# Thresholds of a build-time scheduler set for each period, and the last rows of x transposed on TensorE, in an attention kernel

## The chip, the cores and the metric

The kernel runs on one core of one Trainium2 chip. The time is that of the device in microseconds (us); a profile, taken in one execution, has a span from the first to the last instruction, which is a little shorter than the time. Engines are named as in the profile: PE is TensorE (PEld its weight loads), DVE is VectorE, ACT is ScalarE, POOL is GpSimd, SP is SyncE, which here only issues transfers.

## The reference

Two attention blocks over the same input are mixed by a gate. Block A is full attention with 32 heads of 16 over 2048 rows; block B looks only at 8 earlier rows, two apart.

```python
x = A_x                                            # 1 x 2048 x 512, bf16
g = sigmoid((x * gate_w).sum(-1, keepdims=True))
# block A: q, k, v = x @ wqkv, 32 heads of 16
scores = einsum("bhqd,bhkd->bhqk", q, k) * 16 ** -0.5
a = (softmax(scores) @ v) @ A_wo
# block B: window of W = 8, dilation 2
idx = pos[:, None] - arange(8)[None, :] * 2        # masked where negative
b = (softmax(q . k[idx]) . v[idx]) @ B_wo
return g * a + (1 - g) * b
```

Block A has 32 x 2048 x 2048 scores, each of which needs an exponential. That is the bulk of the work.

## The kernel before

The program is written by a small planner that runs while the kernel is built. It keeps a time for each engine, estimates how long each step takes, and emits each instruction at the moment when its plan would start it. On the chip each engine then runs its own list in this order. The planner's thresholds therefore decide the order of instructions, and nothing else.

Block A is cut into 32 periods: 4 chunks of 512 queries times 8 groups of 4 heads. A period has 64 units; a unit is one head, 128 keys, 512 queries. TensorE writes scores of 3 or 2 units by turns into a ring in PSUM, ScalarE exponentiates the ring into `pT`, and TensorE adds the product with v to `acc`:

```python
want = 3 if k % 2 == 0 else 2                 # units of ring k
...
def f():                                      # TensorE: the scores
    shut = acc_open[0]
    twice = (shut is not None and not any(row_left[shut])
             and P.have(P.now + dur) < TWICE * P.HAM)
    for _ in range(1 + twice):                # issued twice where TensorE would be thin
        for s_, (p_, t, j) in enumerate(units):
            qk_mm(ring[:, s_, :], p_, t, j)
    ...                                       # and a rider for DVE or POOL, if there is room
# ScalarE:
A.activation(out=st["pT"][:, 0:n, :], in_=ring[:, 0:n, :], func=ACT.Exp,
             scale=LN2 / 128.0, bias=-VOFF * LN2 / 128.0)
```

Some units ("riders") go to a PSUM bank `w` instead, and VectorE computes their exponential in four passes (`ta`, `ta`, `ta`, `pd`), or GpSimd does (`psc`). What ScalarE doesn't exponentiate, these do.

The jobs between the rings (projections of q, k and v, block B, output) may start on TensorE only if they end before ScalarE's queue runs out:

```python
refill = 0.52
RAMP = 0.01
JW = 0.8
JP = 3.0
EARLY = 0.3
TEARLY = 110

def limit(self, st):          # when ScalarE's queue runs out, less refill
    return max(self.free["act"], st) + sum(y[4] for y in self.ready["act"]) + self.coming - self.refill

def room_for_job(self, x, st):
    return not self.calm or st - x[7] > self.JP or self.dve_work(st) >= self.JW

def fits(self, x, st):
    if x[0] < 2 or self.spent or self.free["act"] + 3.0 < st or self.urgent(x):
        return True
    give = self.EARLY if st < self.TEARLY else 0.0
    return st + x[4] - self.limit(st) <= max(give, self.RAMP * (st - x[7] - self.CALM))
```

`URG = 28` tells with how many units left a job of the next period becomes urgent, `DV_MIN = 12` with how few left no rider is taken, `TWICE = 0.60` below which occupancy of TensorE a ring is issued twice at the end of a period. In gaps of TensorE the planner also puts fills: matmuls of zeros, added to `acc`, which change nothing in the result.

At the start x is needed transposed (`xT`). Three chunks of 512 rows are loaded plainly and transposed by TensorE (`s<-ident,xr`), with a copy by DVE or ACT; the fourth is loaded by a transposing transfer:

```python
load_x(8, 4)
SP.dma_start_transpose(out=xT[:, :, 3 * QW:S], in_=x2d[3 * QW:S, :])
SP.dma_start(out=wv[:], in_=a_w3[:, :, 2 * D:3 * D])
...
XDVE = ((1, 0), (1, 0), (1, 1))               # which half is copied by DVE
XARR = ((5.8, 5.8), (7.2, 7.2), (9.3, 9.3), (12.6, 12.6))    # planned arrival, us
...
v_group(0, 8, ev_start[0], 3)                 # v of heads 0 to 7, from the start of period 0
```

Then the first period needs: k of all chunks, the maximum of k (`kmax`), a selector from it (`selk`), a matmul with it, `qt`, and the first ring.

Of the kernel before, what the change touches and what calls it, by code (L numbers as in the profile page):

```python
# [20 lines left out]
NG = 8  # L21
W = 8
DIL = 2
QW = 512
# [27 lines left out]
class Plan:  # L52
# [13 lines left out]
    held = {"job": 0}  # L66
    streamed = deque()
    cap_job = 2
    refill = 0.52
    patience = 6.0  # L70

    def resource(self, name, n):
# [106 lines left out]

    DEFER = 0.0  # L180
    coming = 0.0
    RAMP = 0.01
    CALM = 4.0

    def limit(self, st):
        return max(self.free["act"], st) + sum(y[4] for y in self.ready["act"]) + self.coming - self.refill

    passes = 0
    calm = False
    JW = 0.8  # L190
    JP = 3.0
    HUNG = 0.0
    EARLY = 0.3
# [31 lines left out]
    def run(self):  # L225
        while True:
            best = None
            for e, lst in self.ready.items():
                rs = []
                for x in lst:  # L230
                    g_ = self.gate(x[6])
                    if g_ is not None:
                        rs.append(max(x[2], g_))
                if rs:
                    st = max(self.free[e], min(rs))
                    if best is None or st < best[0]:
                        best = (st, 1, e)
            for r, lst in self.reqs.items():
                if lst and self.slots[r]:
                    st = max(min(x[0] for x in self.slots[r]), min(x[2] for x in lst))  # L240
                    if best is None or st <= best[0]:
                        best = (st, 0, r)
            if best is None:
                return
            st, kind, nm = best
            self.now = st
            if kind == 0:
                lst = self.reqs[nm]
                x = min(y for y in lst if y[2] <= st + 1e-9)
                lst.remove(x)  # L250
                s = min(y for y in self.slots[nm] if y[0] <= st + 1e-9)
                self.slots[nm].remove(s)
                self.advance(x[3], st, s[1])
            else:
                lst = self.ready[nm]
                ok = [y for y in lst if y[2] <= st + 1e-9 and self.gate(y[6]) is not None
                      and self.gate(y[6]) <= st + 1e-9]
                x = min(ok, key=lambda y: (y[0], y[1]))
                if nm == "pe" and 1 <= x[0] < 1.5 and st - x[2] < self.DEFER:
                    jobs = [y for y in lst if y[0] >= 2 and y[4] > 0.5 and y[7] <= st  # L260
                            and self.gate(y[6]) is not None and self.gate(y[6]) <= st + 1e-9]
                    y = min(jobs, key=lambda y: (y[0], y[1])) if jobs else None
                    if (y is not None and st + y[4] <= self.limit(st)
                            and (y[6] != "w" or self.room_for_job(y, st))):
                        x = y
                if nm == "pe" and self.feed_dve(st):
                    continue
                if nm == "pe" and x[6] == "w" and not self.room_for_job(x, st):
                    x[2] = max(x[2], st + 0.1)
                    continue  # L270
                if nm == "pe" and not self.fits(x, st):
                    for y in ok:
                        y[2] = max(y[2], st + 0.1)
                    continue
                lst.remove(x)
                if nm == "pe":
                    self.idle_fill(st, 1 + (x[6] is not None))
                if x[6] is not None:
                    slot = self.take(x[6], st)
                    self.held["job"] += x[6] == "w"  # L280
                    more = x[5](slot)
                else:
                    more = x[5]()
                if isinstance(more, float):
                    x[4] += more
                if nm == "pe":
                    self.stream(st, x[4] - 0.116 - self.thin)
                    self.thin = 0.0
                if CFG_DEBUG:
                    LOG.append((st, x[4], nm, getattr(x[3], '__name__', '?'), x[0]))  # L290
                self.free[nm] = st + x[4]
                self.advance(x[3], st + x[4] + self.LAT[nm], None)


@with_exitstack
def kernel(
# [12 lines left out]
    x2d = A_x.flatten_outer_dims()  # L309
    out2d = out.flatten_outer_dims()  # L310
    S, D = x2d.shape
    assert D == 512 and S == 2048
    NT = S // 128
    NC = S // QW
# [41 lines left out]
    SP = Chained(nc.sync, "sp")  # L356
# [16 lines left out]
    xT = const.tile([128, DC, S], BF16, name="xT")  # L373
# [24 lines left out]
    def load_x(t0, n):  # L398
        SP.dma_start(out=xr[t0 // 8][:, t0 // 4 % 2, t0 % 4:t0 % 4 + n],
                     in_=x2d[t0 * 128:(t0 + n) * 128, :].rearrange("(t p) n -> p t n", p=128))  # L400
# [2 lines left out]
    load_x(4, 4)  # L403
    SP.dma_start(out=wqr[:, :, 0:128], in_=a_w3[:, :, 0:128])
    load_x(8, 4)
    SP.dma_start_transpose(out=xT[:, :, 3 * QW:S], in_=x2d[3 * QW:S, :])
    SP.dma_start(out=wv[:], in_=a_w3[:, :, 2 * D:3 * D])
    SP.dma_start(out=wkr[:, :, 128:D], in_=a_w3[:, :, D + 128:2 * D])
    SP.dma_start(out=wqr[:, :, 128:D], in_=a_w3[:, :, 128:D])
# [41 lines left out]
    P = Plan(["pe", "act", "dve", "pool", "sp"])  # L451
# [24 lines left out]
    QR = 2  # L476
    QRD = 2
    SOLO = 1
    TWICE = 0.60
    THIN = 0.40  # L480
    KRP = 4
    QRP = 3
    XDVE = ((1, 0), (1, 0), (1, 1))
    XARR = ((5.8, 5.8), (7.2, 7.2), (9.3, 9.3), (12.6, 12.6))
    WARR = (4.8, 8.0)
    GP = 4.5
    BB = 3
    BR = 1
    URG = 28
    TURN = 6.0  # L490

    class Bank:
# [17 lines left out]
    NP = len(periods)  # L510
    pidx = {p: k for k, p in enumerate(periods)}
    ev_x = [Event() for _ in range(NC)]
# [6 lines left out]
    ev_q = [Event() for _ in range(NP)]  # L519
    ev_start = [Event() for _ in range(NP)]  # L520
# [16 lines left out]

    def x_job(sc):
        left = [2]
        if sc == NC - 1:  # L540
            yield ("delay", XARR[sc][0])
            yield ("set", ev_x[sc])
            return
        for hf in range(2):
            yield ("spawn", x_half(sc, hf, left))

# [305 lines left out]
    nset = [0]  # L852
    ndve = [0]
    nsolo = [0]
    DV_MIN = 12
    DV_END = 7
    flying = [0]
    psc = [None]
# [54 lines left out]
    def urgent(x):  # L913

        p = front[0]
        return (p < NP - 1 and x[0] <= 4.0 + 0.3 * min(p + 1, 2 * NG) + 0.1 and rem(p) < URG
                and x[3].__name__ in ("k_job", "q_job", "kpk_job", "qpk_job", "v_job"))
    P.urgent = urgent

    def rem(p):  # L920
        return sum(len(d) for d in pend[p])

    def ready(ev, t):
        return ev.time is not None and ev.time <= t
# [86 lines left out]
    def act_stream():  # L1011
        while front[0] < NP:
# [6 lines left out]
            p = front[0]  # L1019
# [16 lines left out]
            for p_, us in parts:  # L1036
                yield ("wait", ev_q[p_])
                for t, j in us:
                    yield ("wait", ev_k[periods[p_][1]][t // TPC])
                if ev_start[p_].time is None:  # L1040
                    P.calm = 0 < p_ < NP - 1
                    yield ("set", ev_start[p_])
            if k == 0:
                next_phase("rA", "rB")
            ring = pools[rname].tile([128, 3 if k % 2 == 0 else 2, QW], FP32, tag=rname, bufs=1, name="ring")
            dur = 0.108 + MM

            def f():
                shut = acc_open[0]
                twice = (shut is not None and not any(row_left[shut])  # L1050
                         and P.have(P.now + dur) < TWICE * P.HAM)
                for _ in range(1 + twice):
                    for s_, (p_, t, j) in enumerate(units):
                        qk_mm(ring[:, s_, :], p_, t, j)
                more = MM * twice
                if (shut is not None and any(row_left[shut])
                        and P.have(P.now + dur) < THIN * P.HAM):
                    more += fill_pass(0.2134, P.now) + 0.01
                js = [u[2] for u in units]
                while len(js) < 4:  # L1060
                    r = rider(js)
                    if r is None:
                        break
                    p_, t, j, s, ds, hs = r
                    js.append(j)
                    wt = wtile(s, [128, QW])
                    qk_mm(wt[:], p_, t, j)
                    P.spawn(vec_unit(p_, t, j, s, ds, hs, wt, ndve[0]), P.now + dur + more + P.LAT["pe"])
                    ndve[0] += 1
                return float(more)  # L1070
# [7 lines left out]
        now = yield ("now",)  # L1078
# [23 lines left out]
    def rider(js, now=None):  # L1102
        now = P.now if now is None else now
        for p in (front[0], front[0] + 1):
            if p >= NP or rem(p) < (DV_MIN if p < NP - 1 else DV_END) or not ready(ev_q[p], now):
                continue
            c_, i = periods[p]
            opts = [j for j in range(4) if j not in js and pend[p][j] and ready(ev_k[i][pend[p][j][-1] // TPC], now)
# [526 lines left out]
    def v_group(h0, h1, rel, prio):  # L1635
        n = (h1 - h0) * DH
        TB = 512 // n
        for tb in range(0, NT, TB):
            P.spawn(v_job(h0, h1, tb, TB, rel, prio + 0.01 * tb))
# [12 lines left out]
        P.spawn(k_job(0, NC - 1, None, 1.5, hf))  # L1652
    P.spawn(sel_job(0, 1.5))
    P.spawn(q_job(0, None, 1.6))
    v_group(0, 8, ev_start[0], 3)
    P.spawn(act_stream())
    P.spawn(g_job(GP))
    P.spawn(psc_job(ev_lent), 16.0)
# [18 lines left out]
    for c_ in range(NC):  # L1677
        for b in range(NB):
            p = pidx[(c_, 2 * b + 2)]
# [58 lines left out]
```

## Time and profile before

| | before |
|---|---|
| time, median of 3 runs | 849.57 us (849.07 to 849.78) |
| span of the profile | 848.0 us |
| PE busy | 751.2 us, 89% |
| DVE busy | 762.1 us, 90% |
| ACT busy | 826.6 us, 97% |
| POOL busy | 725.3 us, 86% |
| mean granted clock of TensorE | 0.999 |

Busy times overlap: all engines run beside each other, and the shares are of one span. Groups of instructions are named by what they write and read, so `pT<-ring` is an exponential of a ring. A number after the arrow in square brackets, or after the second bar of a group, is the time for which the engine sat idle just before, with what ended it.

### The profile page before, as it was taken

To read this page: it belongs to the slowest core of one execution; us is meant where nothing else is said; L and a number is where in the kernel's file an instruction comes from. 1 tells how busy PE (TensorE), PEld (TensorE's weight loads), DVE (VectorE), ACT (ScalarE), POOL (GpSimd) and SP (SyncE) were. 2 spreads that over 40 slices of the span, in tenths; PEclk is the share of its full clock that TensorE was granted. 3 is DMA by queue.
4 is the path that set the end of the run, shared out by engine and by line. 5 is a ranking of instruction groups with operands and counts; after the bars stand their busy time and mean duration, and the time that the engine had idled before them with its cause. 6 is when DMAs were issued, how large, how long until landed. Compare 5 with 4: busy or idle time off the path is not lost.

```text
span 848.0 us, 15723 instructions
## 1 busy us (share of the span) xinstructions
PE 751.2 (89%) x5813; PEld 267.4 (32%) x5864; DVE 762.1 (90%) x1323; ACT 826.6 (97%) x750; POOL 725.3 (86%) x734
## 2 busy tenths in 40 slices
PE   9999998998898898888899988888888899788887
PEld 4423333342232333222323323332332332233332
DVE  4689799999999999999987899999999989999986
ACT  5999999999999999999999999999999999999996
POOL 2566798989799979899999999999999998988773
PEclk9999999999999999999999999999999999999999
DMA  9000540250434040603041414120313222020100
GB/s 272 29 2 27 167 128 12 84 172 20 131 93 151 13 137 8 180 20 111 14 144 44 131 26 131 57 69 20 106 33 112 75 83 80 20 63 7 14 1 26
DMA packets 74125, 63.84 MB, mean 75 GB/s; under 512 B 22576, under 2 KB 70704, under 8 KB 74048
## 3 DMA queue, kind: packets, MB, share of 16 engines
q1 hardware_dynamic: 72848, 62.57, 24.3%
q8 instruction: 46, 0.75, 0.4%
q10 hardware_dynamic: 1200, 0.26, 0.2%
q14 instruction: 31, 0.25, 0.1%
HBM read 45.61 MB, written 12.62 MB: 69 GB/s over the span
## 4 chain that ended last, share of the span: by engine, by line
ACT 66%; issue 20%; PE 10%; DVE 4%; POOL 0%; ACTq 0%; POOLq 0%
ACT pT L350 65%; PE w L350 4%; PE acc L350 3%; PE ring L350 3%; DVE ta L350 2%; ACT lg L350 1%; PE s L350 1%; DVE pd L350 1%; PE e L350 0%; DVE psc L350 0%; DVE xT L350 0%; DVE d L350 0%; DVE kt_all L350 0%; DVE osb L350 0%; DVE omg L350 0%
## 5 line engine op out<-in xcount | busy, mean ns | idle before, releaser
L350 ACT ACTIVATE pT<-ring 128x1536 bf16<-128x1536 f32 x718 | 817.2, 1408 | 5.2 <-PE acc L350 2.4
L350 PE MATMUL ring<-qt,kt_all 32*128 32x512 bf16 x1860 | 286.9, 381 | 83.1 <-ACT pT L350 69.1
L350 DVE SCALAR_TENSOR_TENSOR ta<-ta,w 128x512 f32<-128x512 f32 x472 | 314.4, 682 | 5.8
L350 POOL TENSOR_TENSOR prod<-prod 128x512 f32<-128x512 f32 (+1 forms) x208 | 240.2, 1166 | 5.7
L350 PE MATMUL acc<-pT,vp_all 128*17 128x512 bf16 x1795 | 221.5, 383 | 2.6 <-DVE accS L350 2.0
L350 PEld LDWEIGHTS <-kt_all 32*128 32x128 bf16 x2113 | 113.2, 91 | 334.7 <-issue 321.8
L350 PE MATMUL acc<-ident,z 128*17 128x512 bf16 (+3 forms) x770 | 193.6, 338 | 1.4 <-POOL ident masks.py:199 1.4
L350 DVE TENSOR_SCALAR ta<-w 128x512 f32<-128x512 uint16 x236 | 161.3, 687 | 37.2 <-PE w L350 35.1
L350 DVE SCALAR_TENSOR_TENSOR pd<-ta,w 128x512 uint16<-128x512 f32 x236 | 159.4, 681 | 3.0
L350 POOL TENSOR_TENSOR prod<-ksh,qb 128x512 f32<-128x512 bf16 x128 | 145.2, 1156 | 2.0
L350 POOL TENSOR_TENSOR prod<-vsh,lg 128x512 f32<-128x512 bf16 x128 | 136.5, 1098 | 2.5
L350 PE MATMUL w<-qt,kt_all 32*128 32x512 bf16 x253 | 95.0, 383 | 0.0
L350 PE MATMUL acc<-pd,vp_all 128*17 128x512 bf16 x253 | 82.0, 380 | 0.0
L350 PEld LDWEIGHTS <-z 128*17 128x17 bf16 (+1 forms) x775 | 53.4, 92 | 71.0 <-issue 43.2
L350 PEld LDWEIGHTS <-vp_all 128*17 128x17 bf16 x2048 | 41.1, 88 | 94.2 <-issue 92.9
L350 POOL TENSOR_TENSOR psc<-psc 128x512 f32<-128x512 f32 x51 | 60.8, 1193 | 3.9
L350 POOL TENSOR_SCALAR psc<-psc 128x512 f32<-128x512 uint16 (+1 forms) x34 | 21.0, 618 | 45.0 <-DVE psc L350 42.8
L350 PE MATMUL w<-bw,xT 128*128 128x512 bf16 x173 | 48.7, 382 | 1.2
L350 PEld LDWEIGHTS <-xT 128*128 128x128 bf16 x448 | 31.6, 98 | 28.1 <-issue 14.6
L350 POOL TENSOR_TENSOR lg<-lg,mx 128x256 f32<-128x256 f32 x16 | 10.1, 629 | 22.1 <-DVE mx L350 22.1
L350 DVE CAST kvs<-w 128x512 bf16<-128x512 f32 x32 | 21.9, 683 | 2.4 <-PE w L350 2.3
L350 DVE COPY accS<-acc 128x512 f32<-128x512 f32 (+1 forms) x33 | 21.9, 667 | 1.9 <-PE acc L350 1.9
(108 smaller groups left out, 447.0 us busy)
## 6 DMA issues: line engine op xcount, KB each, us to landing
ksh<-kv_scr SPq DMA_DIRECT2D x16, 1024.0 KB
vsh<-kv_scr SPq DMA_DIRECT2D x16, 1024.0 KB
kv_scr<-kvs SPq DMA_DIRECT2D x16, 256.0 KB
kt_all<-k_scr SPq DMA_DIRECT2D x6, 512.0 KB
q_scr<-qpk SPq DMA_DIRECT2D x24, 128.0 KB
qt<-q_scr SPq DMA_DIRECT2D x24, 128.0 KB
out_dram<-osb SPq DMA_DIRECT2D x14, 128.0 KB
xr<-in_A_x_dram SPq DMA_DIRECT2D x3, 512.0 KB
```

Of the source, the lines that this page charges most:

```text
L350: return chain_on(self._key, f(*a, **k))
```

## The change

The thresholds are now set anew when a period starts in the plan, from a table with one row for each of the 32 periods. The table was found by a search in the plan: a short end of the plan, with few stretches in which TensorE's occupancy is low. And the last 512 rows of x are loaded plainly, in two halves, and transposed on TensorE like the others. The first group of v no longer waits in the plan for period 0 to start.

```diff
-    refill = 0.52
+    refill = 0.4
...
-    RAMP = 0.01
+    RAMP = 0.006
...
+    TUNED = ("JW", "JP", "RAMP", "refill", "EARLY", "ahead", "least", "shy")
+    ahead = 28
+    least = 12
+    shy = 0.60
...
+STAGES = [
+    (0.8, 3.0, 0.006, 0.4, 0.3, 28, 12, 0.6),
+    (0.8, 3.0, 0.006, 0.4, 0.3, 28, 12, 0.6),
+    (0.8, 3.0, 0.006, 0.4, 0.3, 28, 12, 0.55),
...                                   # 26 rows cut
+    (1.2, 4.0, 0.01, 0.52, 0.3, 28, 10, 0.65),
+    (0.8, 3.0, 0.006, 0.52, 0.3, 36, 14, 0.6),
+    (0.8, 2.0, 0.004, 0.4, 0.3, 32, 10, 0.65),
+]
...
     load_x(8, 4)
-    SP.dma_start_transpose(out=xT[:, :, 3 * QW:S], in_=x2d[3 * QW:S, :])
+    load_x(12, 2)
+    load_x(14, 2)
...
-    XDVE = ((1, 0), (1, 0), (1, 1))
-    XARR = ((5.8, 5.8), (7.2, 7.2), (9.3, 9.3), (12.6, 12.6))
+    XDVE = ((1, 0), (1, 0), (1, 1), (0, 1))
+    XARR = ((5.8, 5.8), (7.2, 7.2), (9.3, 9.3), (9.9, 10.6))
...
-        if sc == NC - 1:
-            yield ("delay", XARR[sc][0])
-            yield ("set", ev_x[sc])
-            return
...
                 if ev_start[p_].time is None:
                     P.calm = 0 < p_ < NP - 1
+                    for nm, v in zip(P.TUNED, STAGES[min(p_, len(STAGES) - 1)]):
+                        setattr(P, nm, v)
                     yield ("set", ev_start[p_])
...
-    v_group(0, 8, ev_start[0], 3)
+    v_group(0, 8, None, 3)
```

`ahead`, `least` and `shy` stand for `URG`, `DV_MIN` and `TWICE` of before.

## The prediction

> **What bounds the kernel now.** I read first the page's busy shares, then the groups with different shapes kept apart, then ScalarE's own timeline at both ends of the span, then the waits, and last the windows for the clock.
>
> ```profile
> span 848.0 us, 15723 instructions
> PE 751.2 (89%) x5813; PEld 267.4 (32%) x5864; DVE 762.1 (90%) x1323; ACT 826.6 (97%) x750; POOL 725.3 (86%) x734
> ACT  5999999999999999999999999999999999999996
> PEclk9999999999999999999999999999999999999999
> ACT 66%; issue 20%; PE 10%; DVE 4%; POOL 0%; ACTq 0%; POOLq 0%
> ```
>
> ScalarE (ACT) is busy in every slice but the first and the last, and the chain that ended last runs through it for 66%. All engines are over 85%, but only ACT has no room.
>
> ```profile
> L350 ACT ACTIVATE pT<-ring 128x1536 bf16<-128x1536 f32 x359 | 581.8, 1621 | 3.6 <-PE ring L350 1.8 <-PE acc L350 1.3 <-PE w L350 0.5
> L350 ACT ACTIVATE pT<-ring 128x1024 bf16<-128x1024 f32 x359 | 429.4, 1196 | 1.6 <-PE acc L350 1.1 <-PE w L350 0.2 <-PE ring L350 0.2
> L350 DVE TENSOR_SCALAR ta<-w 128x512 f32<-128x512 uint16 x236 | 161.3, 687 | 37.2 <-PE w L350 35.1
> L350 POOL TENSOR_SCALAR psc<-psc 128x512 f32<-128x512 uint16 x17 | 10.5, 618 | 43.5 <-DVE psc L350 42.8
> ```
>
> One unit of attention is 128 keys of one head against 512 queries; there are 32 periods x 64 = 2048. ACT exponentiates 359 x 3 + 359 x 2 = 1795 of them, VectorE (DVE) 236 by a polynomial, GpSimd (POOL) 17. The column after the second bar is idle time just before the group: 3.6 + 1.6 = 5.2 us for the whole stream of exponentials.
>
> ```profile
> 14.51 2.56 SPq L350 DMA_DIRECT2D kv_scr<-zpad  x1
> ...
> 17.88 4.62 ACT L350 ACTIVATE pT<-ring 128x1536 bf16<-128x1536 f32 x4 [1.43 <-PE ring L350]
> ```
>
> ```profile
> 818.81 20.45 ACT L350 ACTIVATE pT<-ring 128x1536 bf16<-128x1536 f32 x18 [1.28 <-PE acc L350]
> 842.09 0.37 ACT L350 COPY oT<-e 128x256 bf16<-128x256 bf16 x1 [2.83 <-PE e L350]
> ```
>
> So the span has three parts: a head of 17.88 us before the first exponential, a stream to 818.81 + 20.45 = 839.26, that is 821.4 us, and a tail of 848.0 - 839.26 = 8.7 us. Of the 5.2 us of idle time, 1.43 lies before the first exponential, so the stream holds 3.8 us of idle: one stall of 1.28 at 818 us, and, from ACT's busy time in windows, 1.77 between 40 and 100 us (58.23 busy of 60) and about 0.7 elsewhere. The rate is (821.4 - 3.8) / 1795 = 0.4555 us per unit, small activations included.
>
> [...] ACT's 97% leaves 3.8 us of idle in 821.4[...] The trace has (1621 - 1196) / 512 = 0.83 ns per column[...]; but consecutive activations overlap, since 359 x (1621 + 1196) ns = 1011 us of records fit in 817 us. For this reason I use the 0.4555 us of the stream and not the duration of a record. [...] The granted clock here is 1.00 in every window to 830 us and 0.77 only in the last 3 us, when no matmul is left; so no run of this kernel's stream shows a drop. [...] 0.69 us per copy of 1024 columns on DVE, 1.01 on ACT.
>
> **The change, part by part.** I compared the instruction lists of both programs. Almost all counts are equal; what differs is small.
>
> *The head.* The transposing DMA of the last 512 rows goes: its issue held the SyncE queue from 3.29 for 6.47 us, so that wv was issued at 9.81 us. In its place two plain loads and 16 transposes on TensorE (16 more after the 16 of the third chunk), one copy of 1024 columns on DVE and one on ACT. Was the old transposing load on the path? No: TensorE runs from 13.25 us through the projections of k for chunks 2 and 3 without a gap.
>
> ```profile
> 11.25 1.06 PE L350 MATMUL s<-ident,xr 128*128 128x128 bf16 x16
> 12.15 2.99 PE L350 MATMUL s<-xT,wkp 128*128 128x512 bf16 x16
> 15.07 1.20 PE L350 MATMUL acc<-ident,z 128*32 128x512 bf16 x5
> ```
>
> So this adds one more batch of transposes to a busy engine: 12.15 - 11.25 = 0.90 us later. But 13.25 held a wait for DVE's copy (0.35 us), which the batch covers: +0.6 on TensorE. After this the chain is: k of the last half, its maximum on DVE, the selector, the matmul with it, qt on DVE, the first ring, ACT. The list shows two things put into that chain: 16 matmuls of v (1.07 us in the row at 17.76) now stand ahead of the selector's matmul, and the copy of v on DVE (0.6 us from start to start) stands ahead of qt. I followed it with the durations above, as an estimate: last k projection done at 15.65, last maximum at 16.4, selector 16.85, v matmuls 15.8 to 16.75 and thus beside this, selector's matmul done at 17.3, v's copy 17.0 to 17.6, qt from 17.6 instead of 16.63. qt to ACT's start took 17.88 - 16.63 = 1.25 before, so the first exponential starts at 18.85: **+1.0 us**. For the loads I see no wait: the first three were in by 11.04 and the fourth is needed only at 12.1.
>
> *The units.* DVE's polynomial count goes from 236 to 238, POOL stays at 17, ACT has one activation of 1024 columns less: 2 x 0.4555 = **-0.9 us**. DVE pays 8 passes of 0.6 from start to start (about 4.8 us of its 762), beside ACT.
>
> *The stall at 818 us.* Here two ring refills were issued twice over, and nine products with v and five fills stood ahead of the next ring. Between the ring before and the ring after, 12,288 and 11,264 matmul columns were queued, against a mean of about 7,580 for two rings. In the changed list no such heap is left late (the largest after ring 30 is 10,368). I take the whole stall off: **-1.3 us**.
>
> *The thresholds.* Refill goes from 0.52 to 0.40 in 26 of the 32 rows and RAMP from 0.01 to 0.006 in 23; in eight rows nothing else differs from the old constants, and each other column keeps its old value in 21 to 28 rows. EARLY counts only up to 110 us of the plan, where it is 0.3 as before. A smaller refill lets a projection end 0.12 us later relative to ACT's queue, and a ring takes 17.88 - 17.44 = 0.44 us from its first matmul to ACT's start: 0.40 is a little too tight, and can cost up to 0.04 us where a job just fits. The smaller RAMP takes back a part. Of the other 2.5 us of idle I let 0.4 be won: **-0.3 us** after rounding for the tight fits. Fills fall from 775 to 759 weight loads and second issues by about 5 ring matmuls: off the path.
>
> *The tail.* The matmuls left after the last ring go from 17,920 columns to 16,384, but the last steps are the same chain: 0.
>
> Sum: +1.0 - 0.9 - 1.3 - 0.3 = -1.5, so 849.57 - 1.5 = **848.1 us**.
>
> **Rivals.** *(a) The plan wins nearly all the idle.* If the search has removed the stalls that the plan can see, and the head costs less than I think because loads land early, the gain is up to 3.8 + 0.9 = 4.7 us: 844.9. For it: the change was chosen by the plan's end. Against it: ACT's gaps are few and at different places, 1.77 us of them where EARLY stays, and the head is longer by the list itself. *(b) The clock drops.* [...] ACT starves for some us at each place: 852 to 860. Against it: the clock was 1.00 throughout, and if I count distinct matmul passes against ACT's time in every stretch of four rings, the thinnest is 0.46 before and 0.51 after; the two lists are alike. *(c) TensorE becomes the bound* because jobs may run later into ACT's reserve: small waits of 0.04 to 0.1 us after some of the 718 rings. A hundred of them make +4 to +8 us: 852 to 856. For it: refill below the 0.44 measured. Against it: RAMP is smaller, and 200 rings already waited for ACT, 69.1 us in all, so TensorE is often ahead.
>
> ```profile
> PE ring L350 <- ACT pT L350: 69.1, 200, 0.6
> ACT pT L350 <- PE acc L350: 2.4, 4, 1.3
> ACT pT L350 <- PE ring L350: 2.0, 3, 1.4
> ```
>
> **Range and chances.** Two per cent is 17 us. A gain of that size isn't there: ACT must still do 1793 x 0.4555 = 816.7 us with a head and a tail of 26 us, so 843 + 1.6 (the difference between the time and the span) is about the floor. A loss of 17 us needs rival (b) many times over. Range for 8 in 10: 845.6 (most of rival a) to 851.2 (a part of rival c, or one drop of the clock). Faster by over 2%: 0.01; within 2%: 0.96; slower: 0.03.
>
> **What would show it.** First exponential at 18.6 to 19.2 us, not 17.9. 358 activations of 1024 columns, the stream shorter by 1.5 to 3.5 us, the gap of 1.28 us before a late pT gone, idle before pT in the stream 1.5 to 3.5 us. Clock 1.00 in all windows before the tail. It is wrong if pT's idle before it grows above 5 us with many short waits for ring (rival c), if windows show a clock under 1 (b), or if the head is not longer.

## The result and the profile after

The changed kernel takes 846.57 us (median of 4 runs, 845.55 to 846.89) against 849.57: a ratio of 0.9963, 95% interval 0.9946 to 0.9981. That is 3.0 us less; 848.1 was predicted. The page after, the lines that answer to those of before:

```profile
span 845.0 us, 15726 instructions
PE 747.4 (88%) x5804; PEld 267.3 (32%) x5861; DVE 768.0 (91%) x1332; ACT 826.2 (98%) x750; POOL 725.7 (86%) x734
...
ACT  4999999999999999999999999999999999999996
...
PEclk9999999999999999999999999999999999998999
...
ACT 73%; issue 20%; PE 7%; DVE 0%; POOL 0%; ACTq 0%; POOLq 0%
```

ScalarE is still the bound. New is the 8 in the row of the clock. Next, the exponentials with both shapes apart (busy us, mean ns of a record, idle us just before), and from ScalarE's timeline the pieces of the stream that began after an idle time:

```profile
L391 ACT ACTIVATE pT<-ring 128x1536 bf16<-128x1536 f32 x359 | 588.4, 1639 | 2.6 <-PE ring L391 1.8 <-PE w L391 0.6
L391 ACT ACTIVATE pT<-ring 128x1024 bf16<-128x1024 f32 x358 | 434.8, 1215 | 0.6 <-PE acc L391 0.3
```

```profile
19.10 17.32 ACT L391 ACTIVATE pT<-ring 128x1536 bf16<-128x1536 f32 x15 [1.79 <-PE ring L391]
50.37 75.64 ACT L391 ACTIVATE pT<-ring 128x1024 bf16<-128x1024 f32 x67 [0.32 <-PE acc L391]
774.09 62.57 ACT L391 ACTIVATE pT<-ring 128x1536 bf16<-128x1536 f32 x55 [0.59 <-PE w L391]
```

Idle in the stream is 2.6 + 0.6 - 1.79 (before the first exponential) = 1.4 us, against 3.8. The stall at 818 us is gone, and so are those between 55 and 110 us, which stood so in the timeline of the kernel before:

```profile
59.16 8.23 ACT L350 ACTIVATE pT<-ring 128x1536 bf16<-128x1536 f32 x7 [0.34 <-PE ring L350]
67.57 7.01 ACT L350 ACTIVATE pT<-ring 128x1024 bf16<-128x1024 f32 x6 [0.18 <-PE ring L350]
75.28 14.58 ACT L350 ACTIVATE pT<-ring 128x1024 bf16<-128x1024 f32 x13 [0.70 <-PE acc L350]
90.39 15.12 ACT L350 ACTIVATE pT<-ring 128x1536 bf16<-128x1536 f32 x13 [0.53 <-PE w L350]
105.73 27.23 ACT L350 ACTIVATE pT<-ring 128x1024 bf16<-128x1024 f32 x24 [0.22 <-PE w L350]
```

One new gap stands at 774 us. The windows around it in the changed kernel (length, then busy us of PE, PEld, DVE, ACT, POOL with instructions, granted clock, DMA share, GB/s):

```profile
764.00:768.00 4.00, 3.33 (x29) 0.94 (x29) 3.90 (x7) 4.00 (x4) 3.92 (x4) 1.00 0.01 2
768.00:772.00 4.00, 3.69 (x22) 1.27 (x17) 3.14 (x7) 3.89 (x4) 1.96 (x2) 0.57 0.16 33
772.00:776.00 4.00, 4.00 (x31) 0.84 (x30) 2.42 (x6) 3.28 (x4) 1.01 (x2) 0.58 0.00 0
776.00:780.00 4.00, 3.35 (x29) 1.03 (x29) 3.77 (x7) 4.00 (x4) 3.75 (x4) 1.00 0.00 0
```

For 6.8 us TensorE had half its clock (0.50 in the window from 768.53 to 775.35 us), and ScalarE stood idle for 0.1 + 0.7 us in these windows.

The three parts of the span, and the difference to before: head 19.10 us (+1.22), stream from 19.10 to 836.66, so 817.56 (-3.82), tail 8.34 (-0.40).

### The profile page after: what moved, and what is told of

It reads as the page before. It is cut to its first block, busy times and chain, and to the rows that moved or that the text cites. A ratio compares the mean times of both kernels' runs of the same rounds, so it can differ in the third digit from the quotient of the medians.

```text
span 845.0 us, 15726 instructions
## 1 busy us (share of the span) xinstructions
PE 747.4 (88%) x5804; PEld 267.3 (32%) x5861; DVE 768.0 (91%) x1332; ACT 826.2 (98%) x750; POOL 725.7 (86%) x734
## 4 chain that ended last, share of the span: by engine, by line
ACT 73%; issue 20%; PE 7%; DVE 0%; POOL 0%; ACTq 0%; POOLq 0%
ACT pT L391 72%; PE acc L391 2%; PE ring L391 2%; PE w L391 2%; ACT lg L391 1%; PE s L391 1%; PE e L391 0%; DVE vp_all L391 0%; DVE qt L391 0%; ACT osc L391 0%; POOL ident masks.py:199 0%; ACT e L391 0%; POOL identf masks.py:197 0%; POOL ident masks.py:197 0%; ACTq L391 0%
## 5 line engine op out<-in xcount | busy, mean ns | idle before, releaser
L391 PE MATMUL acc<-ident,z 128*17 128x512 bf16 (+6 forms) x747 | 189.2, 338 | 1.6 <-POOL ident masks.py:199 1.4
L391 PE MATMUL acc<-pd,vp_all 128*17 128x512 bf16 x255 | 84.2, 382 | 0.0
```

The lines of the kernel that those rows point to most:

```text
L391: return chain_on(self._key, f(*a, **k))
```

## The experiments

All kernels are compared by the same reading: "chain" is the time from the first transpose of x on TensorE to the first exponential, "stream" from there to the end of the last exponential, "idle" the idle time of ScalarE within the stream, "rate" (stream - idle) / units. The idle time is summed from the groups above, and good to about 0.1 us. "Units" are those that ScalarE exponentiates: the thresholds decide not only the order, but also how many units go to VectorE and GpSimd instead. "Half clock" tells whether windows of 4 us in the stream of the profiled execution show a clock under 0.98; the lowest of them have 0.50 (e8, e11).

| kernel | median us | chain | stream | units | idle | rate | half clock at |
|---|---|---|---|---|---|---|---|
| before | 849.57 | 10.68 | 821.38 | 1795 | 3.77 | 0.45549 | none |
| changed | 846.57 | 11.70 | 817.56 | 1793 | 1.41 | 0.45519 | 768-776 |
| e1_table_off | 847.84 | 11.70 | 818.50 | 1796 | 1.11 | 0.45512 | none |
| e2_old_load | 845.57 | 11.04 | 816.29 | 1793 | 0.51 | 0.45498 | none |
| e3_old_v_release | 848.15 | 11.34 | 820.18 | 1796 | 2.17 | 0.45546 | 128-132 |
| e4_one_row | 846.08 | 11.70 | 815.87 | 1792 | 0.51 | 0.45500 | none |
| e5_early_v_only | 846.58 | 11.03 | 818.51 | 1796 | 1.11 | 0.45512 | none |
| e6_refill_052 | 848.25 | 11.70 | 818.77 | 1796 | 1.21 | 0.45521 | 732-740 |
| e7_qt_first | 844.99 | 10.68 | 817.86 | 1793 | 1.78 | 0.45515 | 176-184, 636-644 |
| e8_one_row_jw07 | 850.59 | 11.70 | 823.82 | 1793 | 6.31 | 0.45595 | 744-748, 788-804 |
| e9_no_fills | 900.51 | 10.67 | 870.39 | 1793 | 38.57 | 0.46393 | most of the span |
| e10_table_only | 847.32 | 10.68 | 819.41 | 1796 | 1.57 | 0.45537 | none |
| e11_before_jw07 | 849.71 | 10.68 | 824.64 | 1797 | 5.27 | 0.45597 | 228-240 |
| e12_early_v_jw07 | 846.55 | 11.04 | 818.67 | 1795 | 1.41 | 0.45530 | none |

My theory (A) after the result: the table removes the idle time of the stream, the new head is a cost. Rivals: the new load brings the gain (B), the early release of v does (C), the choice per period matters (D), the order is simply sensitive, and a search picks a lucky one (E), and, for the clock, that fills hold it up (F).

**e1_table_off**: the table out, old constants in.

```diff
-                    for nm, v in zip(P.TUNED, STAGES[min(p_, len(STAGES) - 1)]):
-                        setattr(P, nm, v)
-    refill = 0.4                      # and RAMP = 0.006
+    refill = 0.52                     # and RAMP = 0.01
```

> The changed kernel with the table of thresholds taken out: all 32 periods keep the old constants (refill 0.52, RAMP 0.01, the rest as before); the new load of x and the early v stay. The instruction list has 1796 units on ScalarE, three more than the changed kernel. Theory A (the table brings the gain by removing idle time of ScalarE in the stream, and the head costs about 1 us): first exponential at about 19.1 us as in the changed kernel, idle in the stream 2.5 to 4 us, time 848.5 to 850. Theory B (the new load brings the gain, because the weights are issued earlier): time stays within 0.7 us of the changed kernel's 846.6. Theory C (the early v brings it, whatever the thresholds): also within 0.7 us of 846.6.

Measured 847.84 us, ratio to before 0.9988 (0.9981 to 0.9994), first exponential at 19.03. The idle is only 1.11 us, without the table. So A is wrong in claiming all of the idle for the table, and B and C in claiming none of it: the time is 0.5 us above what they allow. Something besides the table takes 2.9 us out of the stream (821.4 to 818.5).

**e2_old_load**: the transposing load back, table and early v kept.

```diff
-    load_x(12, 2)
-    load_x(14, 2)
+    SP.dma_start_transpose(out=xT[:, :, 3 * QW:S], in_=x2d[3 * QW:S, :])
...                                   # XDVE, XARR and x_job as before
```

> The changed kernel with the old load: the last 512 rows of x come by the transposing transfer again, with no transposes on TensorE and no copies for them; table and early v stay. The planner's order from the first ring on is the same as in the changed kernel. Theory A (the new load is a cost in the head): first exponential 0.6 to 0.7 us earlier, at 18.4 to 18.5 us, stream unchanged, time 845.8 to 846.1 against 846.6. Theory B (the new load brings the gain): time 1.5 to 3 us longer than the changed kernel's, 848 to 849.6, through waits for the weights or a longer stream.

Measured 845.57 us, ratio 0.9953 (0.994 to 0.9965). The chain is 11.04 instead of 11.70, 0.66 us as A expected; the first exponential was at 17.77, because the first transpose, too, started 0.67 earlier (6.73 against 7.40): the 17 fills ahead of it on TensorE, the same in both, took less time, the last seven of them 2.42 us against 3.08 (see the last section). B falls: the new load brings nothing that a stream shows. And since the order in the stream is the same as in the changed kernel, instruction by instruction on TensorE, ScalarE, VectorE and GpSimd in the traces, this run also shows what the half clock at 768 us cost (its own windows from 758 to 778 us have 1.00): 817.56 - 816.29 = 1.27 us.

**e3_old_v_release**: the first group of v waits for period 0 again.

```diff
-    v_group(0, 8, None, 3)
+    v_group(0, 8, ev_start[0], 3)
```

> The changed kernel with the first group of v released at the start of period 0 as before; new load and table stay. The list has 1796 units on ScalarE, three more than the changed kernel. Theory A (the table does it): first exponential 0.3 to 0.4 us earlier, 18.7; stream idle as in the changed kernel, 1.4 us; three units more cost 1.4; time about 847.5. Theory C (the early v does it, since without it TensorE has 1 us of work more inside the first period and the later order falls differently): idle in the stream 3 us or more and time 848.5 to 850.

Measured 848.15 us, ratio 0.9988 (0.998 to 0.9996), chain 11.34: the early v costs 0.36 us there. Idle 2.17 us lies between both expectations, and 0.59 of it is at the half clock (0.57 from 128 to 132 us). Neither A nor C alone.

**e4_one_row**: one row for all periods.

```diff
+STAGES = [(0.8, 3.0, 0.006, 0.4, 0.3, 28, 12, 0.6)] * 32
```

> The changed kernel with one row of thresholds for all 32 periods, the one that is most frequent in the table (0.8, 3.0, 0.006, 0.4, 0.3, 28, 12, 0.6). The list has 1792 units on ScalarE, one fewer than the changed kernel. Theory A, in the form that the common shift of refill and RAMP does the work and the choice per period little: within 0.7 us of 846.6. Theory D (the choice per period is what counts, because each row was picked for its period): 848 or more. Either way the clock shows whether more low-occupancy stretches cost anything: the search also looked at these, so this one may have more drops of the clock than the single one of the changed kernel, each worth about 0.8 us.

Measured 846.08 us, ratio 0.9963 (0.995 to 0.9977): the changed kernel's ratio. Without a drop of the clock in its profile the stream is 815.87, against 816.29 of the table. D falls: 32 rows do no better than one, at least than this one, which the search itself chose most often. (In the traces VectorE runs the same order in both up to some 744 us, and ScalarE nearly to the end.)

```profile
L358 ACT ACTIVATE pT<-ring 128x1536 bf16<-128x1536 f32 x358 | 585.9, 1637 | 1.9 <-PE ring L358 1.8
L358 ACT ACTIVATE pT<-ring 128x1024 bf16<-128x1024 f32 x359 | 434.8, 1212 | 0.4 <-PE acc L358 0.3
```

Of these 2.3 us of idle time 1.79 is the head's: half a microsecond is left in the whole stream.

**e5_early_v_only**: the kernel before, with the one line of v.

```diff
-    v_group(0, 8, ev_start[0], 3)
+    v_group(0, 8, None, 3)
```

> The kernel before with one line changed: the first group of v is released at once, and its 16 matmuls go ahead of the first ring; the old load of x and the old thresholds stay. 1796 units on ScalarE; from the first ring on the planner's order is that of e1_table_off. If the parts add up (the new load costs 0.66 us of head, measured from the first transpose to the first exponential): the time is 0.66 us below e1_table_off's 847.84, so 847.2, a stream of 818.5 us and a head of 11.04 us from the first transpose to the first exponential. If the new load has an effect inside the stream as well (weights issued earlier), the stream is longer than 819.5 us and the time 848.5 or more.

Measured 846.58 us, ratio 0.9969 (0.9957 to 0.9981), chain 11.03, stream 818.51: to 0.01 us the stream of e1. One line gives nearly the time of the whole change. Where, is seen in ScalarE's timeline of e5:

```profile
17.66 17.32 ACT L350 ACTIVATE pT<-ring 128x1536 bf16<-128x1536 f32 x15 [1.79 <-PE ring L350]
48.94 75.64 ACT L350 ACTIVATE pT<-ring 128x1024 bf16<-128x1024 f32 x67 [0.32 <-PE acc L350]
306.62 27.23 ACT L350 ACTIVATE pT<-ring 128x1024 bf16<-128x1024 f32 x24 [0.32 <-PE acc L350]
486.80 10.06 ACT L350 ACTIVATE pT<-ring 128x1024 bf16<-128x1024 f32 x9 [0.33 <-PE acc L350]
```

The kernel before had five gaps between 55 and 110 us, 0.34 + 0.18 + 0.70 + 0.53 + 0.22 = 1.97 us, and the one of 1.28 at 818. Both are gone with this line alone; one of 0.32 at 49 us is new.

**e6_refill_052**: the table with the old refill.

```diff
-    (0.8, 3.0, 0.006, 0.4, 0.3, 28, 12, 0.6),     # and so in every row
+    (0.8, 3.0, 0.006, 0.52, 0.3, 28, 12, 0.6),
```

> The changed kernel with refill at its old 0.52 in all periods, the rest of the table kept; 1796 units on ScalarE, three more than the changed kernel, 1.4 us. Rival c of the prediction (0.40 is tighter than the 0.44 us from a ring's first matmul to ScalarE, so the stream of the changed kernel is full of small waits): the rate per unit falls by 0.001 us or more, which gives back 1.8 us, and the time is about 846. Theory A (0.40 costs no measurable waits, it only lets more units go to VectorE and removes stalls): rate per unit unchanged within 0.0005 us, time 847.5 to 848.5.

Measured 848.25 us, ratio 0.9982 (0.9976 to 0.9989); the rate is 0.45521 against 0.45519. So 0.40 makes no small waits that could be measured, and it is 0.40 that lets three more units go to VectorE: rival c of the prediction falls.

**e7_qt_first**: e2 with the copy of the first v behind qt.

```diff
+        if h1 == 8 and tb == 0:
+            yield ("wait", ev_q[0])
         yield ("dve", prio, VP, lambda: V.tensor_copy(out=vp_all[:, tb:tb + TB, h0:h1, 0:DH],
```

> A version built from the findings: table and early v as in the changed kernel, the old load of x, and the first copy of v on VectorE put behind qt, not ahead of it. The order in the stream is that of e2_old_load, 1793 units. If the head's chain is understood: from the first transpose to the first exponential 10.7 us, as in the kernel before (e2_old_load 11.04), and the time 0.35 us below e2_old_load's 845.57, so 845.2. If the copy of v is then late for the first product with v and something else waits: 845.6 or more, with a new gap of ScalarE in the first 10 us of the stream.

Measured 844.99 us, ratio 0.9949 (0.993 to 0.9968). Chain 10.68, that of the kernel before to the hundredth: the head is understood. The profiled execution met two short drops of the clock (windows of 0.60 and 0.97 from 176 us, of 0.70 and 0.87 from 636 us, where e2 has 1.00), and its stream is 1.57 us longer than e2's in the same order. It is the lowest median here, 1.6 us under the changed kernel, but their intervals overlap; what is shown is the head's 1.02 us.

**e8_one_row_jw07**: e4 with one threshold moved by 0.1.

```diff
-STAGES = [(0.8, 3.0, 0.006, 0.4, 0.3, 28, 12, 0.6)] * 32
+STAGES = [(0.7, 3.0, 0.006, 0.4, 0.3, 28, 12, 0.6)] * 32
```

> As e4_one_row, but with JW 0.7 in place of 0.8 in all rows: a threshold on VectorE's planned work moved by 0.1 us. 1793 units on ScalarE, one more than e4_one_row. Theory A (thresholds act smoothly, through the reserve before ScalarE): within 0.7 us of e4_one_row's 846.08. Theory E (the order is sensitive: a small change anywhere makes another order, better or worse by some us, and the search picks a lucky one): another time by 2 us or more, 848 to 851, with stalls of ScalarE in the stream at places where this order puts several jobs ahead of a ring.

Measured 850.59 us, ratio 1.0028 (1.0014 to 1.0042), 4.5 us more than e4; its executions run from 848.97 to 857.02. This is theory E. The late gaps:

```profile
793.21 3.59 ACT L358 ACTIVATE pT<-ring 128x1024 bf16<-128x1024 f32 x3 [0.46 <-PE ring L358]
797.76 2.60 ACT L358 ACTIVATE pT<-ring 128x1536 bf16<-128x1536 f32 x2 [0.96 <-PE ring L358]
800.95 2.45 ACT L358 ACTIVATE pT<-ring 128x1536 bf16<-128x1536 f32 x2 [0.59 <-PE ring L358]
...
823.39 19.53 ACT L358 ACTIVATE pT<-ring 128x1536 bf16<-128x1536 f32 x17 [1.47 <-PE acc L358]
```

Those at 793 to 801 are at half clock (0.50, 0.50 and 0.67 in the windows from 792 to 804 us); that at 823 is at full clock (1.00 from 820 to 828), a heap of products with v ahead of a ring at the change of a period, as before at 818. So both happen: another order, and more drops of the clock (a mean of 0.997 or less in 22 of 22 executions, in e4 in 4 of 6).

**e9_no_fills**: e7 with the fills left out behind the start; the other instructions stay in their order.

```diff
-            mm(acc_tiles[p][32 * j:32 * j + DH + 1, 0:m], z32[:, 0:DH + 1], filling(m), False, False, tile_position=(0, 32 * j))
             done += m
...                                   # and those written to a free bank
```

> The version of e7_qt_first with all fills after the first ring left out (matmuls of zeros, added to acc or written to a free bank; about 730 of them), while every other instruction keeps its place; the result is the same, since the fills add zeros. Theory F (the clock drops where TensorE is thin, and the fills keep it up): mean granted clock 0.95 or lower, many stretches at half the clock, ScalarE's idle in the stream 10 us or more, time 855 to 900. Rival (a drop is chance, and the doubled rings and the real work hold the clock): clock above 0.99 and time within 1.5 us of 845.0.

Measured 900.51 us, ratio 1.0609 (1.0591 to 1.0626). The mean granted clock is 0.778:

```profile
span 897.2 us, 14226 instructions
...
PEclk9998996968796965875999687657677787655577
```

```profile
L391 ACT ACTIVATE pT<-ring 128x1536 bf16<-128x1536 f32 x359 | 538.4, 1500 | 19.6 <-PE ring L391 12.1 <-PE w L391 3.5 <-PE acc L391 1.9
L391 ACT ACTIVATE pT<-ring 128x1024 bf16<-128x1024 f32 x358 | 385.1, 1076 | 20.4 <-PE ring L391 17.0 <-PE w L391 1.3 <-PE acc L391 0.5
```

That is half a microsecond more than the most that theory F named. F stands for the fills behind the start as a whole, and the rival falls: the mean clock is 0.995 in the profile of e7 and 0.778 without them, and the matmuls of zeros are worth 900.51 - 844.99 = 55.5 us here. The search asked for few low-occupancy stretches; what a single one of them costs is not shown by this run.

**e10_table_only**: the kernel before with the table; load and release of v as before. (The diff is the first part of the change.)

> The kernel before with the table of thresholds alone: old load of x, first group of v released at the start of period 0. 1796 units on ScalarE. The order in the stream is that of e3_old_v_release, whose stream had one drop of the clock at 128 to 132 us. If the parts add up: from the first transpose to the first exponential 10.68 us as in the kernel before, 0.66 us less than e3_old_v_release, so the time is 848.15 - 0.66 = 847.5; stream 819.0 us without a drop of the clock, 820.2 with one. If the table needs the early v to do any good: the stream is 821 us as before and the time 849 to 849.5.

Measured 847.32 us, ratio 0.9974 (0.9963 to 0.9985), chain 10.68, stream 819.41 with no drop. The table works without the early v: its gaps between 50 and 80 us sum to 1.04 us against 1.97 between 55 and 110 before, and the stall at 818 us is gone here too. With the old load throughout and no drop of the clock in any of the four profiles, the two parts make this table of streams:

| stream, us (median time) | old thresholds | table |
|---|---|---|
| v from the start of period 0 | 821.4 (849.57) | 819.4 (847.32, e10) |
| early v | 818.5 (846.58, e5) | 816.3 (845.57, e2) |

Early v -2.9, table -2.0, both -5.1: the sums agree, but not term by term. Idle time falls by 2.7 with the early v, by 2.2 with the table and by only 3.3 with both, above all since either alone already takes off the stall at 818 us. The units on ScalarE, on the other hand, rise by one with either and fall by two with both, which is worth 4 x 0.455 = 1.8 us. That the one makes up for the other is luck. And in the medians both together gain 4.0 us and not 3.0 + 2.2: three of the five executions of e2 have a mean clock of 0.995 or less.

**e11_before_jw07** and **e12_early_v_jw07**: JW 0.7 for 0.8 in the kernel before and in e5, old thresholds otherwise, to see whether the early v helps in another order.

```diff
-    JW = 0.8
+    JW = 0.7
```

> The kernel before with one threshold moved, JW 0.7 in place of 0.8; 1797 units on ScalarE, two more than before, 0.9 us. Theory E (the order is sensitive, so a threshold moves the time by some us either way): the time differs from 849.5 by more than the 0.9 us of the units, and the stalls at 59, 75, 90 and 818 us lie elsewhere. If thresholds act smoothly: 850.0 to 850.7 with stalls at the same places.

> The same with the first group of v released at once (e5_early_v_only with JW 0.7); 1795 units. If the early v takes 1 us of TensorE work out of a first period that is short of it, the gain shows here too: 2.5 us or more below e11_before_jw07, and none of the stalls between 55 and 110 us. If its gain in e5_early_v_only was only a luckier order: no gain over e11_before_jw07, or stalls between 55 and 110 us as in the kernel before, about 1.5 us or more.

Measured 849.71 (1.0005, 0.9997 to 1.0013) and 846.55 (0.9972, 0.9961 to 0.9982): 3.2 us apart. In e11 the early gaps lie where they lay before (57.9 to 104.5 us, 1.96 in all); they are the same gaps, for its order on TensorE is that of the kernel before up to 206 us. The two of 1.06 and 1.02 us at 234 and 238 are at half clock (0.50 and 0.52 in the windows from 232 to 240 us), and the stall at 818 us is gone. The last piece of the stream without idle time, of e10 and then of e11:

```profile
749.67 86.60 ACT L391 ACTIVATE pT<-ring 128x1536 bf16<-128x1536 f32 x77
769.00 72.25 ACT L350 ACTIVATE pT<-ring 128x1024 bf16<-128x1024 f32 x64
```

In e12 the early gaps are not quite gone, though that was expected; they have shrunk to 0.17 + 0.27:

```profile
48.82 25.14 ACT L350 ACTIVATE pT<-ring 128x1024 bf16<-128x1024 f32 x22 [0.32 <-PE acc L350]
74.12 12.32 ACT L350 ACTIVATE pT<-ring 128x1024 bf16<-128x1024 f32 x11 [0.17 <-PE acc L350]
86.71 44.39 ACT L350 ACTIVATE pT<-ring 128x1536 bf16<-128x1536 f32 x39 [0.27 <-PE w L350]
```

The order of e12 leaves that of e5 at 54 us, so this is a second order in which the early v nearly clears that stretch; a third is that of the changed kernel. So the early v was no accident of one order. And JW, which cost 4.5 us in e8, cost nothing in these two: theory E is not the rule but a risk.

## Why the prediction was right, and where it was not

The direction, the small size and the range hold; the gain was 3.0 us and not 1.5. Term by term:

- *Head, +1.0.* Right. The order costs 11.70 - 10.68 = 1.02 us, 0.66 by the transposes and copies (e2) and 0.36 by v's copy ahead of qt (e3, e7). The other 0.2 of the 1.22 is not the order's: the 17 fills ahead of the first transpose took 6.02 us against 5.82.
- *Units, -0.9.* Right: 1793 units, 358 activations of 1024 columns.
- *The stall at 818 us, -1.3.* Right in size; as to the cause, the table alone takes it off (e10), but so do the early v alone (e5) and JW 0.7 alone (e11). It was a stall of one order.
- *The thresholds, -0.3.* This is the term that failed: "Of the other 2.5 us of idle I let 0.4 be won". In the changed kernel 1.1 is won, although a drop of the clock cost 0.9 of idle time in its profile; in the same order without a drop (e2) it is 2.0. And instead of the tight fits that I charged, the rate improved from 0.45549 to 0.45519, 0.5 us over 1793 units. (The rate rises with the idle time down the table, to 0.46393 where that is 38.57 us, so this may be a part of the same stalls and not a gain of its own; no run separates the two.)
- *The tail, 0.* It is 0.4 shorter; no run here isolates it.

The measured terms sum: +1.0 + 0.2 - 0.9 - 1.3 - 1.1 - 0.5 - 0.4 = -3.0.

Behind the failed term lies a step I did not take. I saw the 16 matmuls of v move ahead of the first ring, priced what they cost there, and did not ask what their going leaves behind. TensorE has 1.07 us less to do in a stretch in which the planner lets jobs run into ScalarE's reserve (EARLY, up to 110 us), and there the gaps were. That stretch is where the gaps vanish (e5) or shrink (e12); that the room is the reason is argued from this, not shown by itself. The stall at 818 us needs no such reason: of the other orders with fills, that of e8 has one of its kind (1.47 us at 823), that of e6 has 0.15 us at 818, and the rest have none in the last 60 us of the stream. So its going tells nothing of the table in particular.

Rival (a) was nearest: most of the idle was won, though not by a cheaper head. Rival (b) happened on a small scale. Its 852 to 860 us was my estimate, from no trace: the profile of the kernel before has no drop in its stream to work it out from. I took the clock of one profile of the kernel before, and the likeness of the two lists, as evidence that the new order is safe; that thin stretches decide where the clock drops was assumed, not shown. The new order is less safe: a mean clock of 0.997 or less stands at 4 of 4 executions of the changed kernel, and at 4 of the 110 of the kernel before that were measured beside the experiments. A drop costs less than the "some us at each place" of the prediction: 1.27 us of stream for 6.8 us at 0.50 (changed against e2), and 1.57 for the two in e7 together, which come to about 6.9 us at 0.50 (an estimate from the four windows given there). And "1.00 in every window" holds for the stream alone: at the start, as from 3 to 7 us in the changed kernel, the windows say 1.00 although the first clock on record is at 7.36 us (last section). Rival (c) fell with e6.

## What to carry to other kernels

When work moves out of a busy stretch, price both ends: what it costs where it now stands, and what the stretch that it left can do with the room. Cut a span into head, stream and tail, and divide the stream by the units of the engine that bounds it; then a change of 0.3% can be followed term by term, which the time alone (its runs spread by 1 us and more) does not allow. A table of thresholds found by a search should be set against one row: here it did no better, and the one line beside it did about as much. The search also looked for few stretches of low occupancy, and yet the clock drops more often (a mean of 0.997 or less in 4 of 4 executions against 4 of 110): the clock of all executions is to be compared, not that of one profile.

## What was not expected of the hardware

- The clock of TensorE drops at different places, or nowhere, for one and the same order of instructions: none in e2, windows of 0.57 and 0.58 at 768 to 776 us in the changed kernel, 0.60 at 176 and 0.70 at 636 us in e7. How often it drops differs between orders: 4 of 110 executions before, 4 of 4 changed, 1 of 9 in e12 and 22 of 22 in e8 have a mean of 0.997 or less. Without fills the mean is 0.778 in the profile of e9, against 0.995 in that of e7.
- The first transpose of x started between 5.93 us (e11) and 7.40 us (changed) after the span's start: 1.5 us, half of the change's gain. It does not wait for its load, the last part of which had landed by 5.1 us in e11 and 5.4 in the changed kernel, but for the 17 fills ahead of it on TensorE, the same in all kernels. In e11 and then in the changed kernel:

```profile
1.45 4.55 PE L350 MATMUL acc<-ident,z 128*32 128x512 bf16 x17 [1.45 <-POOL ident masks.py:199]
1.44 6.02 PE L391 MATMUL acc<-ident,z 128*32 128x512 bf16 x17 [1.44 <-POOL ident masks.py:199]
```

  After the first few they follow each other at 0.43 us, in e11 at 0.22 us from 4.4 us on. The trace's first record of the full clock is at 4.36 us in e11, at 6.93 before (first transpose at 7.20) and at 7.36 in the changed kernel; over the 14 profiles, the later it is, the later the first transpose starts.
- The record of an exponential can be the longer one where ScalarE is better fed: 128x1536 took 1639 ns by its record in the changed kernel (idle in the stream 1.41 us), 1621 before (3.77) and 1500 in e9 (38.57). In the changed kernel 359 x 1639 + 358 x 1215 ns = 1023 us of records lie in a stream of 817.56 us: they overlap, so their mean is no price.
